# Fused attention, routed experts and a dense layer on one core: head 1's parts written in place, loads moved in the MoE

## The chip, the cores and the metric

The kernel runs on one core of a Trainium2 chip. Five engines with their own instruction streams share the work: TensorE (PE; its weight loads are shown apart as PEld), VectorE (DVE), ScalarE (ACT), GpSimd (POOL) and SyncE (SP), which here does little but issue DMAs and load registers. The metric is the device time of one execution in microseconds; the median of three executions counts.

## What is computed

Attention with rotary embedding, then a routed layer (each token goes to the best of 8 experts, chosen by the gate and a bias), then a dense layer with a gate of its own. Cut to what matters:

```python
B, H, S, D = 2, 8, 576, 64                      # 1152 tokens of 512
q, k = rotate(q), rotate(k)
attn = softmax(q @ k.T / sqrt(D)) @ v
x = attn.transpose(0, 2, 1, 3).reshape(1152, 512)
e = argmax(x @ w_gate + modality_bias[modality_id])
for each expert i, its tokens m:                # w1 8x512x1024, w2 8x1024x512
    x[m] = gate[m] * (relu(x[m] @ w1[i]) @ w2[i])
h = x @ w_in                                    # 512x2048
g = h * tanh(log1p(exp(min(h, 20))))            # h where h > 20
out = g @ w_out                                 # 2048x512
```

## The kernel before

**Arithmetic.** A float32 operand is split into a high part in the format that TensorE multiplies at full rate (`F32R`) and a low part, the rest. ScalarE or GpSimd copies the high part, VectorE or GpSimd subtracts it from the value for the low one, and a product is the sum of three matmuls (high x high, low x high, high x low). In the names `...h` or `hi` is the high part, `...l` or `lo` the low one.

**Attention** takes 16 heads `n`. For each, a load `xs` holds q (64 partitions) and k (64 partitions) with a copy of them that has its halves swapped; `p_mul` (L900) multiplies by the table of cosines and sines, `p_add` (L908) adds, `p_hi` (L920) and `p_lo` (L924) write the parts into a buffer `ab`, and `p_stack` (L930) copies `ab` with four DMAs into `sq` (q's parts above each other) and `sk` (k's parts, each on both halves of the partitions). Head 0 has a path of its own (`p_first`), in which ScalarE and VectorE write `sq` and `sk` without DMAs. Then come the scores `sc` (L963), their maximum (L973), the exponential `pexp` (L984), its transposes `pt` (L997), the parts `ph` (L1017) and `pl` (L1023), the product with v, `av` (L1038), and `xo` (L1068), which places the result in `X`. One of a head's tiles of queries is half of head n+1, so that head 0 needs head 1's `sq` and `sk`. The order of all instructions is made by the class `Plan`: a list scheduler with a key for every operation (table `K`), a cost, and counted buffers (`slots`). Of `xs` there are two buffers, and head 1's and head 2's loads come first; the scheduler has a choice of two engines for most preparing operations.

**Routing and MoE.** Each of the two batch halves `b` is routed (L313 to L524): places of the tokens are counted, GpSimd scatters the rows of `X` to a sorted array `scratch` (L408), and a table `tbl` gives for each tile its expert and first row. SP loads these numbers into registers (`tile_regs`, L552). A tile has up to 304 tokens of one expert; `moe_tile` (L673) loads 8 chunks of the expert's weights (`wraw`, L590, 0.5 MB each), ScalarE and GpSimd split them into `whi` (L598) and `wlo` (L603), and TensorE multiplies (L695). There are two tiles for each half, (0, 0), (0, 1), (1, 0) and (1, 1), and a loop L1381 over extra tiles, whose number `nxi` (L549) is computed by VectorE and loaded into a register of every engine by L1378; here it is zero and the loop's body does not run.

**The order in the MoE** comes from three generators that are advanced against each other. `pump` (L1263) advances the tiles of half 0 by `P['rq']` us of matmuls for every VectorE step of the routing of half 1. That routing ends with the register loads of the tiles of half 1, and then `merge_extra` (L526) ends with `nxi` and the DMA of `ei` into `extra`. `drive` (L1347) then runs on: `P['vl']` matmuls ahead of the register load of `nxi`, and 41 after it ahead of the loop. In `drive`, VectorE gets one decoding piece after every 24 matmuls.

**Decoding.** The dense layer's weights arrive as 16 blocks `wr` of 1 MB (`dec_load`, L1289, two buffers), of 64-bit numbers. VectorE decodes each in three pieces (L1296, L1301, L1306) into `wc`. After the third piece of block f, block f+2 is loaded:

```python
            next(d)
            if f + 2 < FC2:
                dec_load(f + 2)
```

All DMAs named here are issued by SP, one after the other in program order; an issue that waits holds those behind it.

**The last stage** takes the 16 blocks for 640 tokens and then for 512. TensorE makes `h` (L1453), ScalarE and VectorE the gate (L1464 to L1476, with a reciprocal at L1475), ScalarE and GpSimd its parts `g`, and TensorE the product `o` (L1510). The rest of the decoding pieces stand between the reciprocals.

## Time and profile before

| | before |
|---|---|
| Median of three executions | 522.54 us (521.99 to 524.20) |
| The profiled execution | 523.88 us |
| Its span, first to last instruction | 522.2 us |
| Mean granted clock of TensorE | 0.977 of full |
| Busy: TensorE, VectorE, ScalarE, GpSimd | 480.7, 409.8, 332.4, 366.3 us |

In the trace, attention ends near 172 us, the first two MoE tiles near 243, the other two near 304, and the last stage runs to the end. Busy time of TensorE is modelled for pipelined matmuls, so the time of a row of many matmuls is read from their number in a stretch. The granted clock of 1.00 is 2.4 GHz, and a stretch at the lower level shows 0.50 (1.2 GHz).

### The profile page before, as it was taken

The page shows a single profiled execution, that of the slowest core. Times are in us where ns is not written, and L with a number is a line of the kernel's source. Part 1 is how long each engine was busy: PE and PEld are TensorE (multiplying, and loading weights), DVE is VectorE, ACT ScalarE, POOL GpSimd, SP SyncE. Part 2 cuts the span into 40 slices and gives each one's busy share as a digit, 9 for nine tenths or more (in the row PEclk, how much of TensorE's full clock was granted, in tenths as well). Part 3 has the DMA queues.
Part 4 walks back from the last instruction along what each step waited for, and adds up shares of the span by engine and source line. Part 5 has one row for each costly group of instructions (what it writes and reads, how often), then busy time and mean ns, then how long its engine had stood idle before and what let it go on. Part 6 is the DMA issues. An engine that isn't in the chain of part 4 may idle for free.

```text
span 522.2 us, 9092 instructions
## 1 busy us (share of the span) xinstructions
PE 480.7 (92%) x3152; PEld 444.8 (85%) x3152; DVE 409.8 (78%) x586; ACT 332.4 (64%) x750; POOL 366.3 (70%) x359
## 2 busy tenths in 40 slices
PE   2699999999999979898999988899999899999995
PEld 1589999998988869897989987789898789999994
DVE  6489888898887665481696889999999967877773
ACT  2388788767869515454464475666666568776763
POOL 4889989999833355664777665677778558977664
PEclk9999999999999979899999999999999899999998
DMA  6588976777633684683875522022220000100001
GB/s 210 140 193 228 229 204 171 208 185 206 140 122 130 203 313 158 225 310 121 282 247 203 211 82 81 1 81 82 80 82 2 1 2 40 49 14 1 1 1 81
DMA packets 24131, 69.42 MB, mean 133 GB/s; under 512 B 5522, under 2 KB 9810, under 8 KB 22034
## 3 DMA queue, kind: packets, MB, share of 16 engines
...
q14 instruction: 23, 0.19, 0.1%
...
## 4 chain that ended last, share of the span: by engine, by line
PE 34%; DVE 12%; ACT 2%; issue 2%; POOL 2%; DMA 1%; POOLq 0%; ACTq 0%
PE h L1453 13%; PE o L1510 13%; PE mm L695 7%; DVE ta L1475 6%; DVE wc L1306 1%; DVE wc L1301 1%; DMA wraw(1, 0)_5_3587<-in_w_dram 1%; DVE yl L1401 1%; DVE ta L1476 1%; POOL wlo(1, 0)_2_3552 L603 1%; POOL wlo(1, 0)_1_3542 L603 0%; ACT w2h L1436 0%; PE mm L661 0%; DVE wc L1296 0%; POOL out_dram L1520 0%
## 5 line engine op out<-in xcount | busy, mean ns | idle before, releaser
L1475 DVE RECIPROCAL ta<-ta 128x320 f32<-128x320 f32 (+1 forms) x64 | 124.7, 1948 | 22.0 <-ACT ta L1468 20.7
L1493 POOL TENSOR_TENSOR g<-ta,g 128x320 fp32r<-128x320 f32 (+1 forms) x63 | 60.1, 954 | 61.4 <-issue 29.0
L1510 PE MATMUL o<-w2h,g 128*128 128x512 f32 x288 | 101.0, 398 | 0.0
L1437 POOL TENSOR_TENSOR w2l<-wc,w2h 128x512 fp32r<-128x512 f32 x64 | 85.7, 1360 | 3.5 <-ACT w2h L1436 3.5
L1453 PE MATMUL h<-yh,w2h 128*128 128x320 f32 (+1 forms) x256 | 76.4, 299 | 6.2 <-DVE ta L1476 6.2
L1453 PE MATMUL h<-yh,w2l 128*128 128x320 f32 (+1 forms) x256 | 76.2, 298 | 0.6 <-POOL w2l L1437 0.6
L1453 PE MATMUL h<-yl,w2h 128*128 128x320 f32 (+1 forms) x256 | 75.9, 297 | 0.2 <-DVE yl L1401 0.2
L963 PE MATMUL sc<-sk,sq 128*128 128x288 f32 (+1 forms) x320 | 59.8, 320 | 15.4 <-ACT sk L890 9.4
L984 ACT ACTIVATE pexp<-sc,nm 128x576 f32<-128x576 f32 x72 | 53.3, 741 | 24.2 <-DVE nm L973 19.3
L973 DVE TENSOR_REDUCE nm<-sc 128x1 f32<-128x576 f32 x72 | 53.5, 751 | 14.6 <-PE sc L963 11.0
L1510 PEld LDWEIGHTS o<-w2h,g 128*128 128x128 f32 x288 | 54.5, 190 | 11.0 <-POOL g L1493 1.0
L963 PEld LDWEIGHTS sc<-sk,sq 128*128 128x128 f32 (+1 forms) x320 | 47.6, 195 | 17.7 <-ACT sk L890 9.4
L1017 ACT ACTIVATE ph<-pt 128x512 fp32r<-128x512 f32 (+2 forms) x112 | 54.6, 510 | 12.2 <-PE pt L997 11.6
L1453 PEld LDWEIGHTS h<-yh,w2h 128*128 128x128 f32 x256 | 48.4, 189 | 11.1 <-DVE ta L1476 7.8
L997 PE MATMUL pt<-ident,pexp 128*128 128x128 f32 (+1 forms) x360 | 54.9, 278 | 2.7 <-DVE pl L1023 1.8
L1510 PE MATMUL o<-w2l,g 128*128 128x512 f32 x144 | 57.2, 397 | 0.0
L1487 ACT ACTIVATE g<-ta 128x320 fp32r<-128x320 f32 (+1 forms) x64 | 27.9, 436 | 41.7 <-DVE ta L1476 41.6
L1023 DVE TENSOR_TENSOR pl<-pt,ph 128x512 fp32r<-128x512 f32 (+1 forms) x80 | 48.9, 628 | 3.0 <-ACT ph L1017 2.6
L1038 PE MATMUL av<-ph,vhl 128*128 128x256 f32 (+1 forms) x160 | 50.9, 334 | 0.4 <-ACT avt L1047 0.2
L1453 PEld LDWEIGHTS h<-yl,w2h 128*128 128x128 f32 x256 | 48.3, 189 | 2.6 <-DVE yl L1401 0.4
L1453 PEld LDWEIGHTS h<-yh,w2l 128*128 128x128 f32 x256 | 48.3, 189 | 0.8 <-POOL w2l L1437 0.8
L997 PEld LDWEIGHTS pt<-ident,pexp 128*128 128x128 f32 (+1 forms) x360 | 42.1, 138 | 5.7 <-issue 2.0
...
## 6 DMA issues: line engine op xcount, KB each, us to landing
wr<-in_wio_dram SPq DMA_DIRECT2D x16, 1024.0 KB, 4.8
...
```

What stands on the lines that cost most here:

```text
L963: nc.tensor.matmul(t[:m, hf, :NC2], lhsT=sq[:, c:c + m], rhs=sk[:, z, hf * NC2:(hf + 1) * NC2], start=(z == 0), stop=(z == 1),)
L973: nc.vector.tensor_reduce(out=nm[n, j], in_=sc[n, j][:, :, :NC2], axis=AX.XY, op=ALU.max, negate=True)
L984: nc.scalar.activation(out=pe, in_=sc.pop((n, j))[:, :, :NC2], func=AF.Exp, bias=nm.pop((n, j)), accum_out=st[n, hf][:, i:i + 1],)
L997: nc.tensor.transpose(out=t[:kn, o:o + 128], in_=pexp[n, j][:, k0:k0 + kn], identity=ident)
L1017: nc.scalar.activation(out=block(ph, n, hf, kts, slice(0, kn)), in_=psum(n, hf, kts, kn), func=AF.Copy)
L1023: nc.vector.tensor_tensor(out=block(pl, n, hf, kts, slice(0, 128)) if kn == 128 else block(ph, n, hf, kts, slice(64, 128)), in0=psum(n, hf ...
L1038: nc.tensor.matmul(av[n, hf][:, :u.nq], lhsT=vhl[n][:, kt].rearrange("p a d -> p (a d)"), rhs=src[:, kt, u.at:u.at + u.nq], start=(kt == 0 ...
L1437: nc.gpsimd.tensor_tensor(out=lo[:, cs], in0=w[:, cs], in1=hi[:, cs].bitcast(F32), op=ALU.subtract)
L1453: nc.tensor.matmul(ps[:, :w], lhsT=wt[:, c], rhs=m[g, i][:, c], start=(n == 0), stop=(n == 11))
L1475: nc.vector.reciprocal(out=ta, in_=ta)
L1493: eng.tensor_tensor(out=gt[q][1][:, o:o + w], in0=tas.pop((q, i))[:, :w], in1=gt[q][0][:, o:o + w].bitcast(F32), op=ALU.subtract,)
L1510: nc.tensor.matmul(acc[g, t], lhsT=a[:, s], rhs=b, start=(f == 0 and z == 0), stop=(f == FC2 - 1 and z == 2),)
```

## The change

It has three parts.

**Head 1 in place.** For n = 1 alone, `p_hi`, `p_lo` and the four stacking DMAs are replaced. `d_hi` copies three parts on ScalarE (k, q, and `t`, which is k's second place), `d_lo` subtracts the three low parts on VectorE (GpSimd is the planner's other choice), all straight into `sq` and `sk`. `xs` gets a third buffer, free from the start, so that head 3's load is issued early.

**Register loads.** The two constants of `P` change, SP's register loads of the tiles of half 1 and the `extra` DMA move out of the routing and of `merge_extra`, and stand after a further `drive` of 24 matmuls; another 24 follow ahead of the register load of `nxi`.

**Loads of `wr`.** Until the last stage a freed buffer's load is only noted in `due`, and issued 16 matmuls after the decoding piece that freed it. From the last stage on it is issued at once.

```diff
-P = {... 'vl': 9, ... 'rq': (0.45, 0.47, 0.2), ...}
+P = {... 'vl': 24, ... 'rq': (0.52, 0.55, 0.25), ...}
...
-        nc.sync.dma_start(out=extra.rearrange("(o r) c -> o r c", o=1), in_=ei)
+        cur["ei"] = ei
...
-                [128, 2, S], F32, tag="xs" if n else "ab", name=f"xs{n}", bufs=2 if n else 1
+                [128, 2, S], F32, tag="xs" if n else "ab", name=f"xs{n}", bufs=3 if n else 1
...
+        def d_hi(n, part, eng="act"):
+            if n not in qk:
+                d_new(n)
+            sq, sk = qk[n]
+            r = slice(0, 64) if part == "q" else slice(64, 128)
+            out = {"q": sq[0:64], "k": sk[64:128, 0], "t": sk[0:64, 0]}[part]
+            if eng == "act":
+                nc.scalar.activation(out=out, in_=xin[n][r, 0], func=AF.Copy)
+            else:
+                nc.vector.tensor_copy(out, xin[n][r, 0])
+
+        def d_lo(n, part, eng="dve"):
+            sq, sk = qk[n]
+            r = slice(0, 64) if part == "q" else slice(64, 128)
+            out = {"q": sq[64:128], "k": sk[64:128, 1], "t": sk[0:64, 1]}[part]
+            hi = sq[0:64] if part == "q" else sk[64:128, 0]
+            lo_eng[eng].tensor_tensor(
+                out=out, in0=xin[n][r, 0], in1=hi.bitcast(F32), op=ALU.subtract
+            )
...
-             ... "xs": [], ...
+             ... "xs": [0.0], ...
...
-                op("phi", ("pool", "act"), (0.74, 0.573), z + pr[1], p_hi, n, deps=[("add", n)],
-                   take=[("ab", n)])
-                op("plo", ("pool", "dve"), (1.36, 0.669), z + pr[2], p_lo, n, deps=[("phi", n)],
-                   give=[("xs", n)])
-                op("stack", "sp", 2.5, z + pr[3], p_stack, n, deps=[("plo", n)], take=[("qs", n)],
-                   give=[("ab", n)], tail=2.3)
+                if n == 1:
+                    for part in "kqt":
+                        op("dhi", "act", 0.53, z + pr[1], d_hi, n, part, deps=[("add", n)],
+                           take=[("qs", n)] * (part == "k"))
+                    for part in "kqt":
+                        op("dlo", ("dve", "pool"), (0.669, 1.36), z + pr[2], d_lo, n, part,
+                           deps=[("dhi", n, "q" if part == "q" else "k")])
+                    plan.op(("stack", n), "sp", 0.0, z + pr[3], lambda: xin.pop(1),
+                            deps=[("dlo", n, x) for x in "kqt"] + [("dhi", n, "t")],
+                            give=[("xs", n)])
+                else:
+                    op("phi", ("pool", "act"), (0.74, 0.573), z + pr[1], p_hi, n, deps=[("add", n)],
+                       take=[("ab", n)])
+                    op("plo", ("pool", "dve"), (1.36, 0.669), z + pr[2], p_lo, n, deps=[("phi", n)],
+                       give=[("xs", n)])
+                    op("stack", "sp", 2.5, z + pr[3], p_stack, n, deps=[("plo", n)], take=[("qs", n)],
+                       give=[("ab", n)], tail=2.3)
...
     def route(b):
         yield from routing(b, lambda: cur["rbank"]())
-        if b:
-            tile_rows(b)
...
+    due, behind = [], [True]
+
+    def flush():
+        while due:
+            dec_load(due.pop(0))
...
-                dec_load(f + 2)
+                due.append(f + 2)
+                if not behind[0]:
+                    flush()
...
+                if nq_[0] % (3 * every) == 2 * every:
+                    flush()
...
+        drive(gen0, P["dec"][0], P["d0"], P["vl"])
+        tile_rows(1)
+        nc.sync.dma_start(out=extra.rearrange("(o r) c -> o r c", o=1), in_=cur["ei"])
...
+        behind[0] = False
+        flush()
```

The order of the instructions shows where this lands. GpSimd at the start, before, from its add of head 1 (`xs_124`) on; `xs_130` is head 2, `ab_196` the buffer that is stacked for head 1, `vhl_223` a part of v:

```order
L910 TENSOR_TENSOR xs_124<-xs_124 128x576 [waits Pool_49]
L916 TENSOR_SCALAR ab_196<-xs_124 128x576 [waits DVE_49,Pool_49]
L925 TENSOR_TENSOR ab_196<-xs_124,ab_196 128x576 [waits Pool_49]
L916 TENSOR_SCALAR vhl_223<-vraw_128 128x5x64 [waits DMAHW0_49]
L910 TENSOR_TENSOR xs_130<-xs_130 128x576 [waits DVE_49]
L1056 TENSOR_SCALAR rs_1_249<-stt 128x2 [waits Activation_49]
L916 TENSOR_SCALAR vhl_251<-vraw_187 128x5x64 [waits DMAHW4_49]
```

And after, with the parts of head 1 gone and the multiplication of head 2 (L904 of `xs_130`) come in, which VectorE did before:

```order
L910 TENSOR_TENSOR xs_124<-xs_124 128x576 [waits Pool_49]
L916 TENSOR_SCALAR vhl_198<-vraw_128 128x5x64 [waits DMAHW0_49]
L904 TENSOR_TENSOR xs_130<-xs_130,tabs 128x1152 [waits DMAHW1_49]
L910 TENSOR_TENSOR xs_130<-xs_130 128x576 [waits Pool_49]
L1082 TENSOR_SCALAR rs_1_256<-stt 128x2 [waits DVE_49,Activation_49]
L916 TENSOR_SCALAR ab_258<-xs_130 128x576 [waits DVE_49,Pool_49]
L925 TENSOR_TENSOR ab_258<-xs_130,ab_258 128x576 [waits Pool_49]
```

VectorE at the same place after the change, from the maxima of the first scores on: `xs_173` is head 3, whose multiplication stands where head 2's was before, and `sk_207` and `sq_206` are head 1's, written by the three new subtractions (L962):

```order
L999 TENSOR_REDUCE nm_4_187<-sc_111 128x1 [waits PE_49]
L999 TENSOR_REDUCE nm_3_191<-sc_110 128x1
L904 TENSOR_TENSOR xs_173<-xs_173,tabs 128x1152 [waits DMAHW4_49]
L999 TENSOR_REDUCE nm_0_214<-sc_110 128x1 [waits PE_49,Activation_49]
L962 TENSOR_TENSOR sk_207<-xs_124,sk_207 64x576 [waits DMAHW5_49,Activation_49]
L962 TENSOR_TENSOR sq_206<-xs_124,sq_206 64x576 [waits Activation_49]
L962 TENSOR_TENSOR sk_207<-xs_124,sk_207 64x576
L999 TENSOR_REDUCE nm_1_241<-sc_111 128x1 [waits PE_49]
L1049 TENSOR_TENSOR pl_1_233<-pt_1_0_209,ph_1_232 128x512 [waits Activation_49]
```

The maximum `nm_1` and the low parts `pl` now stand behind these subtractions. TensorE, before, from the transposes of head 0 to the first scores of head 1 (`sk_233`):

```order
L997 MATMUL pt_1_4_229<-ident,pexp_4_194 64x128
L1038 MATMUL av<-ph_1_215,vhl_170 128x256 [waits DVE_49,Activation_49]
L1038 MATMUL av<-pl_1_216,vhl_170 128x256 [waits DVE_49]
L1038 MATMUL av<-ph_1_215,vhl_170 128x256
L1038 MATMUL av<-pl_1_216,vhl_170 128x256
...
L1068 MATMUL xo_1_265<-mov,avt_114 128x72 [waits DMAHW3_49,DMAHW2_49,Activation_49]
L1068 MATMUL xo_1_265<-mov,avt_114 128x72
L963 MATMUL sc_110<-sk_233,sq_232 128x288 [waits DMAHW6_49,DMAHW7_49,DMAHW5_49,DMAHW0_49]
L963 MATMUL sc_110<-sk_233,sq_232 128x288
```

And after, where the scores of head 1 (`sk_207`) stand ahead of all `av` and of `xo`:

```order
L1023 MATMUL pt_1_4_229<-ident,pexp_4_196 64x128
L989 MATMUL sc_110<-sk_207,sq_206 128x288 [waits DVE_49,Activation_49]
L989 MATMUL sc_110<-sk_207,sq_206 128x288 [waits DVE_49]
L989 MATMUL sc_110<-sk_157,sq_156 64x288 x2
L989 MATMUL sc_110<-sk_207,sq_206 128x288 x2
L989 MATMUL sc_110<-sk_157,sq_156 64x288 x2
L1064 MATMUL av<-ph_1_232,vhl_170 128x256
L1064 MATMUL av<-pl_1_233,vhl_170 128x256 [waits DVE_49]
```

So nine `av` and four `xo` matmuls went behind the first scores of head 1.

SP in the MoE, before: the loads of `tbl` are the register loads of the second half's tiles, which stand between `wraw(0, 0)_5` and `_6`:

```order
L1289 DMA wr_2697<-in_wio_dram 128x2048 [waits DVE_49]
...
L590 DMA wraw(0, 0)_5_2708<-in_w_dram 128x1024 [waits DMAHW7_49,DVE_49]
L554 TENSOR_LOAD tbl_2743 [waits DVE_49]
...
L555 TENSOR_LOAD tbl_2743
...
L1289 DMA wr_2792<-in_wio_dram 128x2048
...
L590 DMA wraw(0, 0)_6_2801<-in_w_dram 128x1024 [waits DMAHW0_49,DVE_49]
L550 DMA extra<-ei 1x32 [waits DVE_49]
L1378 TENSOR_LOAD nxi [waits DVE_49]
...
L590 DMA wraw(0, 0)_7_2863<-in_w_dram 128x1024 [waits DMASW6_49,DMASW7_49,DMASW5_49,DMAHW1_49,DMASW1_49,DMASW0_49]
...
L590 DMA wraw(0, 1)_0_2908<-in_w_dram 128x1024 [waits DMAHW2_49,DVE_49,PE_49]
L1289 DMA wr_2956<-in_wio_dram 128x2048 [waits DMAHW4_49,DMAHW3_49,DVE_49]
...
L590 DMA wraw(0, 1)_1_2970<-in_w_dram 128x1024
```

And after, where each `wr` stands one chunk later or two, and the register loads behind chunk 7:

```order
L590 DMA wraw(0, 0)_5_2696<-in_w_dram 128x1024 [waits DMAHW3_49,DVE_49]
L1324 DMA wr_2715<-in_wio_dram 128x2048
...
L590 DMA wraw(0, 0)_6_2749<-in_w_dram 128x1024 [waits DMAHW4_49,DVE_49]
L1324 DMA wr_2784<-in_wio_dram 128x2048
...
L590 DMA wraw(0, 0)_7_2802<-in_w_dram 128x1024 [waits DMAHW0_49,Pool_49]
L554 TENSOR_LOAD tbl_2766 [waits DVE_49]
...
L555 TENSOR_LOAD tbl_2766
...
L1419 DMA extra<-ei 1x32 [waits DMAHW5_49,DVE_49]
...
L590 DMA wraw(0, 1)_0_2893<-in_w_dram 128x1024 [waits DMASW6_49,DMASW7_49,DMASW5_49,DMAHW6_49,DMASW1_49,DMASW0_49]
L1426 TENSOR_LOAD nxi [waits DVE_49]
...
L590 DMA wraw(0, 1)_1_2966<-in_w_dram 128x1024 [waits DMAHW7_49,DVE_49,PE_49]
...
L590 DMA wraw(0, 1)_2_2999<-in_w_dram 128x1024
```

TensorE's own register load of `nxi`, before, inside the products of chunk 3:

```order
L695 MATMUL mm_2808<-xh(0, 0)_2507,wlo(0, 0)_3_2643 128x304
L695 MATMUL mm_2808<-xh(0, 0)_2507,whi(0, 0)_3_2641 128x304
L695 MATMUL mm_2808<-xl(0, 0)_2508,whi(0, 0)_3_2641 128x304
L1378 TENSOR_LOAD nxi [waits DVE_49]
L695 MATMUL mm_2808<-xh(0, 0)_2507,wlo(0, 0)_3_2643 128x304
```

And after, 55 matmuls further on, inside those of chunk 5:

```order
L695 MATMUL mm_2899<-hh(0, 0)_2577,whi(0, 0)_5_2751 128x304
L695 MATMUL mm_2899<-hl(0, 0)_2578,whi(0, 0)_5_2751 128x304
L1426 TENSOR_LOAD nxi [waits DVE_49]
L695 MATMUL mm_2899<-hh(0, 0)_2577,wlo(0, 0)_5_2753 128x304
L695 MATMUL mm_2899<-hh(0, 0)_2577,whi(0, 0)_5_2751 128x304
```

## Rows read from the trace of the kernel before

**Rows 1.** Stretches: from:to, us; busy of PE, PEld, DVE, ACT, POOL; clock, DMA.

```profile
180.00:185.00 5.00, 5.00 (x39) 5.00 (x38) 4.73 (x18) 2.22 (x4) 3.47 (x5) 1.00 1.00 342
190.00:195.00 5.00, 5.00 (x22) 5.00 (x21) 1.90 (x4) 0.85 (x2) 2.37 (x1) 0.51 0.71 277
215.00:220.00 5.00, 4.68 (x22) 4.68 (x23) 3.01 (x5) 1.22 (x2) 5.00 (x3) 0.66 0.67 193
320.00:400.00 80.00, 76.29 (x419) 67.37 (x418) 79.28 (x69) 48.60 (x112) 53.80 (x43) 1.00 0.19 66
```

**Rows 2.** TensorE in order of time: start, us, operation, count, [idle before <-releaser].

```profile
19.35 0.56 PE L1038 MATMUL av<-ph,vhl 128*128 128x256 f32 x1
...
21.99 0.67 PE L1068 MATMUL xo<-mov,avt 128*128 128x72 f32 x4 [0.47 <-ACT avt L1047]
24.46 3.25 PE L963 MATMUL sc<-sk,sq 128*128 128x288 f32 x12 [1.81 <-DMA sk<-ab]
28.46 0.80 PE L963 MATMUL sc<-sk,sq 128*128 128x288 f32 x4 [0.76 <-ACT pexp L984]
...
189.42 0.59 PE L695 MATMUL mm<-xh(0, 0)_2507,wlo(0, 0)_3_2643 128*128 128x304 f32 x1 [3.71 <-DVE nxi L549]
```

**Rows 3.** Waits of TensorE, whole span: us in total, times, longest.

```profile
PE h L1453 <- DVE ta L1476: 6.2, 5, 1.8
...
PE mm L695 <- POOL wlo(0, 1)_1_3007 L603: 1.9, 1, 1.9
```

**Rows 4.** VectorE in order of time.

```profile
9.21 1.52 DVE L893 TENSOR_TENSOR sk<-xs,sk 64x576 fp32r<-64x576 f32 x2
...
188.44 0.14 DVE L549 TENSOR_TENSOR nxi<-nx,nx 1x1 int32<-1x1 f32 x1
...
278.78 2.40 DVE L1301 SCALAR_TENSOR_TENSOR wc<-wr,wc 128x1024 int32<-128x1024 int32 x1
```

**Rows 5.** DMA issues of SP in order of time.

```profile
204.13 0.34 SPq L1289 DMA_DIRECT2D wr<-in_wio_dram  x1
```

**Rows 6.** ScalarE in order of time.

```profile
8.71 0.68 ACT L890 ACTIVATE sk<-xs 64x576 fp32r<-64x576 f32 x1
...
188.92 1.06 ACT L598 ACTIVATE whi(0, 0)_5_2803<-wraw(0, 0)_5_2708 128x1024 fp32r<-128x1024 f32 x1 [4.27 <-DMA wraw(0, 0)_5_2708<-in_w_dram]
...
211.77 1.06 ACT L598 ACTIVATE whi(0, 1)_1_3005<-wraw(0, 1)_1_2970 128x1024 fp32r<-128x1024 f32 x1 [5.06 <-DMA wraw(0, 1)_1_2970<-in_w_dram]
```

**Rows 7.** Waits of SP's queue, 155 to 310 us: total, times, longest.

```profile
SPq L1289 <- DVE wc L1306: 42.8, 9, 10.3
...
SPq L554 <- DVE md L540: 6.8, 1, 6.8
```

**Rows 8.** GpSimd in order of time.

```profile
14.22 2.60 POOL L910 TENSOR_TENSOR xs<-xs 128x576 f32<-128x576 f32 x1
16.91 0.67 POOL L916 TENSOR_SCALAR ab<-xs 128x576 fp32r<-128x576 f32 x1
...
19.05 0.46 POOL L916 TENSOR_SCALAR vhl<-vraw 128x320 fp32r<-128x320 f32 x1
19.47 1.42 POOL L910 TENSOR_TENSOR xs<-xs 128x576 f32<-128x576 f32 x1
...
26.62 2.65 POOL L904 TENSOR_TENSOR xs<-xs,tabs 128x1152 f32<-128x1152 f32 x1
...
187.02 0.97 POOL L408 DMA_INDIRECT scratch<-X,row  x1 [0.22 <-issue]
...
277.70 2.41 POOL L603 TENSOR_TENSOR wlo(1, 1)_2_3882<-wraw(1, 1)_2_3808,whi(1, 1)_2_3880 128x1024 fp32r<-128x1024 f32 x1 [0.93 <-ACT whi(1, 1)_2_3880 L598]
```

**Rows 9.** Decoding pieces, by line: count, ns least/median/most, first and last start.

```profile
L1301 DVE SCALAR_TENSOR_TENSOR wc<-wr,wc x16: 1211/1224/2407, 194.7 to 402.1; 128x1024 int32<-128x1024 int32 x16
L1306 DVE SCALAR_TENSOR_TENSOR wc<-wr,wc x16: 1207/1800/2817, 202.5 to 404.2; 128x1024 int32<-128x1024 int32 x16
```

**Rows 10.** The page's DMA issues: count, KB each, median us to landing.

```profile
wr<-in_wio_dram SPq DMA_DIRECT2D x16, 1024.0 KB, 4.8
```

More of the change, by code (lines that the diff above doesn't have):

```diff
@@ L38 @@
 Q = {'r0': 2.45, 'rd': 2.0, 'tanh': 1.06, 'rec': 1.1, 'hi': 2.2, 'lo': 2.38, 'o': 3.86}
-P = {'sd': (3, 4), 'dl': (28, 44), 'qd': (2, 3), 'alt': (0.1, 4), 'd0': 41, 'vl': 9, 'w3': 3, 'rq': (0.45, 0.47, 0.2), 'dec': (8, 8, 8), 'rl': 3, 'ah': 0, 'eps': 0.05, 'slack': 0.1}
+P = {'sd': (3, 4), 'dl': (28, 44), 'qd': (2, 3), 'alt': (0.1, 4), 'd0': 41, 'vl': 24, 'w3': 3, 'rq': (0.52, 0.55, 0.25), 'dec': (8, 8, 8), 'rl': 3, 'ah': 0, 'eps': 0.05, 'slack': 0.1}
 K = {'ld': -22.67, 'prep': (-24.92, -22.38, -23.33, -27.14, -20.49, -7.62), 'sc': (-8.42, -3.18, 1.68, 1.67, 2.84, 10.44, 1.99, 8.05, 9.75), 'max': (-2.26, -5.46, -1.21, -1.85, 5.06, 8.41, 4.71, 11.42, 13.72), 'exp': (-3.19, 1.66, 6.32, 3.7, 13.26, 11.14, 14.6, -2.87, 25.74), 'tr': (0.69, 2.1, 2.56, 2.68, 5.53, 7.5, 8.45, 9.85, 10.88, 11.85, 15.56, 16.66, 16.92, 19.98), 'hi': (-3.91, -0.31, 2.51, 3.62, 4.25, 4.9, 5.01, 5.32, 7.26, 9.77, 13.56, 14.12, 14.6, 15.66), 'lo': (0.77, 1.83, 5.61, 6.34, 6.67, 7.32, 10.02, 10.73, 12.18, 13.92, 13.94, 14.62, 17.33, 18.02), 'pv': (7.08, 7.84, 10.5, 10.69, 14.13, 14.25, 14.32, 15.96, 18.04, 20.31, 21.03, 22.86, 23.97, 25.61), 'evac': (14.53, 9.65, 6.27, 25.13), 'rec': (-4.7, -0.45, 4.11, 12.71), 'fmm': (4.53, -3.79, 16.24, 17.22), 'norm': (15.5, 16.11, 26.18, 35.69)}
@@ L938, in p_stack, with d_new @@
             qk[n] = (sq, sk)
+        def d_new(n):
+            sq = p2.tile([128, S], F32R, tag="sq", name=f"sq{n}", bufs=3)
+            sk = p2.tile([128, 2, S], F32R, tag="sk", name=f"sk{n}", bufs=3)
+            qk[n] = (sq, sk)
+        def d_hi(n, part, eng="act"):
[16 more added lines that the diff above has]
+            )
         def v_hi(n, eng="pool"):
@@ L1096, in attention @@
             {"sc": [0.0] * 2, "pexp": [0.0] * 5, "ph": [0.0] * 2, "pha": [0.0], "av": [0.0], "qs": [0.0, 8.6],
-             "vhl": [0.0] * 2, "xs": [], "vraw": [11.9], "ab": [0.0], "avt0": [0.0],
+             "vhl": [0.0] * 2, "xs": [0.0], "vraw": [11.9], "ab": [0.0], "avt0": [0.0],
              "avt1": [0.0], "st": [0.0] * 8},
```

## The prediction

> **What bounds the kernel now.** I read the busy time by stretch first [rows 1], then what TensorE waited for [rows 2, 3], then what stood behind each wait. TensorE is the bound nearly everywhere. In an undisturbed stretch of the MoE it runs 39 matmuls of 304 columns in 5 us, 0.13 us each, at a granted clock of 1.00. In three places it is not full, and the change touches all three.
>
> First, the start. TensorE has finished head 0's early work by 22.7 us (nine `av` matmuls from 19.35, then four `xo`) and waits 1.81 us, until 24.46, for the stack DMAs of head 1 [rows 2]. The next twelve score matmuls take 3.25 us where four take 0.80 a little later, which would be 2.40 for twelve: the lower clock. One more wait of 0.76 follows at 28.46.
>
> Second, the MoE's first two tiles. TensorE stands 3.71 us until 189.42 [rows 2] for `nxi`, which VectorE writes at 188.44 [rows 4], and then gets 22 matmuls into 190 to 195, at a granted clock of 0.51, where 39 would go [rows 1]. It stands 1.9 us more for `wlo(0, 1)_1` [rows 3], and 215 to 220 again holds only 22 matmuls, clock 0.66 [rows 1]. The chain behind the second wait begins on SP's queue: the load of `wr` ahead of chunk `wraw(0, 1)_1` is issued at 204.13 [rows 5], the chunk's own right behind it, and ScalarE, idle 5.06 us for the chunk, splits it only at 211.77 [rows 6]. In 155 to 310 us SP stood 42.8 us in all before `wr` loads, for VectorE to free their buffer, and 6.8 us before the register loads of L554 [rows 7]; all that is queued behind these stood too.
>
> Third, the last stage. From 320 to 400 us VectorE is busy 79.28 of 80 us [rows 1], and TensorE's waits for L1476 come to 6.2 us [rows 3]. There VectorE is the bound.
>
> **Part 1, head 1 in place.** Before, GpSimd adds (2.60 us from 14.22, so until 16.82), makes the high part in 0.67 and subtracts [rows 8], and four DMAs stack the parts. Now three ScalarE copies of 64x576 (0.68 each [rows 6]) and three VectorE subtractions (1.52 for two, 0.76 each [rows 4]) write them, with no DMA. By these durations alone the copies run from 16.9 to 18.9 and the last subtraction is done at 19.9. TensorE has other work until 22.7, so the 1.81, the 0.76 and the 0.85 of low clock would all go: -3.4 us. That is the better bound.
>
> I don't take it, because of what GpSimd does meanwhile. The order puts the multiplication of head 2 on GpSimd right behind the add (before, VectorE did it), as one instruction, which takes 2.65 us [rows 8]. The trace shows what becomes of a two-input operation of VectorE while GpSimd is inside one. At 277.70 GpSimd starts a subtraction of 2.41 [rows 8]; VectorE's L1301 starts at 278.78, takes 2.40 and so ends 1.07 after GpSimd does [rows 4], though its median is 1.22 [rows 9]. It waited for the other's end. The opposite shows too: the add at 14.22 took 2.60, with VectorE's multiplication beside it, and the next one 1.42 [rows 8].
>
> The Trainium skill, "SBUF — State Buffer", "Who interferes with whom", has it as a rule: a VectorE instruction with two SBUF inputs and a GpSimd instruction that reads SBUF exclude each other for the whole instruction, and the order of issue decides who blocks. The rows above agree. It speaks against this part of the change: by it the part gives nothing or costs, by the lone durations it gives 3.4.
>
> So, from the rows: GpSimd's piece of `vhl` (0.46 [rows 8]) ends near 17.4, and its multiplication runs from 17.45 to 20.1. The first copy ends at 17.6, so the first subtraction comes too late by 0.2 and runs from 20.1 to 20.9. GpSimd's add for head 2 (1.42) stands ready and goes next, to 22.3; then the second and third subtraction, to 23.8, or 24.5 if GpSimd gets an instruction of 0.67 in between. Head 1 is ready at 23.8 instead of 24.46. But the order now has the nine `av` and the four `xo` behind the first scores of head 1, not ahead of them: 19.35 to 22.7 with a wait of 0.47 inside [rows 2], so 2.8 of work. Before, TensorE was through both at 30.0, which is 24.46 + 5.5, 0.8 of it the wait at 28.46. After: 23.8 + 5.5 - 0.8 + 2.8 = 31.3, and less if the 2.8 does not lie in the low clock as a whole. I take +1.0, with -3.4 (no collision) and +2.0 (third subtraction at 24.5) as bounds. Head 2's parts leave GpSimd no later than before, and the third buffer moves the load of head 3 to where TensorE waits for no DMA; both at nothing, as TensorE asks for head 2 some 9 us after head 1. Should that cover fail, it is inside the +2.0.
>
> **Part 2, register loads and `wr` loads in the MoE.** TensorE's load of `nxi` moves 55 matmuls back, to the end of chunk 5, which is 55 x 0.13 = 7.2 us of its time: 185.7 + 7.2 = 192.9, against 188.6 when the value is there. The 3.71 goes, and with it the low clock after it: 22 instead of 39 matmuls in 5 us, 17/39 x 5 = 2.2. The load itself stays on TensorE: from 188.58, when `nxi` is written [rows 4], to 189.42 it took 0.84, and that is left. What is late next is chunk 5. ScalarE got it only at 188.92, after 4.27 idle for its DMA [rows 6], which was queued behind 1 MB of `wr`, and GpSimd's last scatter ran until 188.0 [rows 8]. In the new order `wraw(0, 0)_5` stands ahead of that `wr`, so its low part is done 2.4 us after the scatter, at 190.5. TensorE comes to it 39 matmuls after the 185.7, at 190.8. That cover is thin, 0.3 us.
>
> SP's register loads of the second tile and the `extra` DMA move behind one `wr` load more and chunks 6 and 7, so these no longer stand behind VectorE. And `wr` loads are issued 16 matmuls after their buffer is free, when SP need not stand for it: `wraw(0, 1)_1` and `_2` are now ahead of the `wr` that they waited behind. The 1.9 goes, and the low clock after it: 22 matmuls in 4.68 us instead of 22 x 0.13 = 2.9, so 1.8. Sum: 3.7 + 2.2 - 0.8 + 1.9 + 1.8 = 8.8. Bounds: 5.1 (only the first wait goes, 3.7 + 2.2 - 0.8) and 9.6 (the load of the register hidden too).
>
> **Part 3, the last stage.** In the new order VectorE has one decoded piece less done when the loop begins, 10 instead of 11, and 26 instead of 27 before the first reciprocal: one more of L1306 in the stretch that VectorE bounds, 1.21 to 2.82 us, median 1.80 [rows 9]. That is +1.8. Bounds: 0, if what TensorE has queued absorbs it, and +4.0, if one of its waits grows so far that the clock falls for another 2.2, as at 190. In that stage the `wr` loads are issued at once, as before.
>
> **Sum.** -8.8 + 1.0 + 1.8 = -6.0 us. The profiled execution took 523.88 us, 1.34 above the median of 522.54 and 1.7 above its own span; 517.9 there, 516.5 at the median.
>
> **Rivals.**
> *The start pays.* If the load of head 3 or the piece of `vhl` shifts the two engines by a few tenths, the first subtraction goes ahead of the multiplication and GpSimd waits instead: -3.4 instead of +1.0, so 512.1. For it: the subtraction is late by only 0.2. Against it: both follow from the same add, which fixes their order.
> *Half of the MoE.* Chunk 5 is covered by 0.3 us, and the DMA engines are full in 180 to 185, share 1.00 at 342 GB/s [rows 1], so a later chunk may be late anyway. If one wait like the second comes back (1.9 + 1.8), the sum is -2.3: 520.2.
> *The register load still waits.* If VectorE writes `nxi` over 4 us later than now, because its routing work is pumped in another rhythm, TensorE waits at the new place and the change does not do what it says: 3.7 + 2.2 come back without the 0.8 and the sum is -0.9, 521.6. Against it: the pumping gets faster, not slower.
> *Slower.* The `wr` loads start 16 matmuls (2.1 us) later. VectorE decodes a third of one every 24 matmuls, 3.1 us, and a buffer that a third piece frees is asked for again three pieces after, 9.4 us. Less the 2.1, that leaves 7.3 us for a landing, median 4.8 [rows 10]. Where landings are longer, the decoding piece blocks VectorE, and queued behind it `hl`, for which TensorE waits. To end over 525.2, 8.7 above my sum, the nine loads that SP stood before [rows 7] would each have to be 1.0 late: landings of 8.3 us. For it: the full DMA engines at 180 to 185. Against it: that is one stretch, not nine.
>
> **How the numbers follow.** The forecast (514 to 519) 0.45; the start pays 0.22; half of the MoE 0.18; register load 0.08; slower 0.07. The range for 8 in 10 goes from 511.5, where the start pays and the MoE gives its 9.6, to 521.5, which leaves out the slower case and part of the register's. About 0.5%, 2.6 us, is what a measurement here can tell from no change: 519.9 to 525.2. Faster by more: 0.45 + 0.22 + 0.08 of the half case = 0.75. Within: 0.10 + 0.08 = 0.18. Slower: 0.07.
>
> **What would show it.** Right: no TensorE wait for `nxi`, clock 1.00 at 190 to 195, no wait for `wlo(0, 1)_1`; the first subtraction of head 1 lasting over 2 us beside GpSimd's multiplication, and head 1's first score at 23.5 to 24.5; the last stage's VectorE as full as now. Wrong: subtractions of 0.76 each and scores of head 1 before 21 (the start pays); a new TensorE wait for a `wlo` of chunks 5 to 7, or for `hl` behind a late decoding piece.

## The result and the profile after

The change takes 516.58 us (median; 515.54 to 518.28) where the kernel before, run beside it, takes 522.26 (519.96 to 524.2): a ratio of 0.9896, 95% interval 0.9867 to 0.9925, or 5.7 us less. The forecast was 516.5. The profiled execution took 515.94, its span is 514.2; before it was 523.88 and 522.2, so the two spans differ by 8.0, more than the medians.

Where the 8.0 went is read by marks that both traces have, in TensorE's and VectorE's order of time (start, us, operation): the first MoE matmul, the first matmul behind the MoE loop, the first reciprocal of the last stage, and the last matmul that waited for VectorE's `ta`. Before:

```profile
172.44 0.41 PE L695 MATMUL mm<-xh(0, 0)_2507,whi(0, 0)_0_2348 128*128 128x304 f32 x1
...
244.84 0.41 PE L695 MATMUL mm<-xh(1, 0)_3274,whi(1, 0)_0_3302 128*128 128x304 f32 x1 [2.07 <-issue]
...
307.51 2.15 DVE L1475 RECIPROCAL ta<-ta 128x320 f32<-128x320 f32 x1 [0.65 <-ACT ta L1468]
...
408.61 0.42 PE L1453 MATMUL h<-yh,w2h 128*128 128x320 f32 x1 [1.77 <-DVE ta L1476]
```

After:

```profile
172.90 0.41 PE L695 MATMUL mm<-xh(0, 0)_2506,whi(0, 0)_0_2338 128*128 128x304 f32 x1
...
236.50 0.41 PE L695 MATMUL mm<-xh(1, 0)_3272,whi(1, 0)_0_3300 128*128 128x304 f32 x1 [2.14 <-issue]
...
298.58 2.15 DVE L1523 RECIPROCAL ta<-ta 128x320 f32<-128x320 f32 x1 [0.65 <-ACT ta L1516]
...
402.52 0.42 PE L1501 MATMUL h<-yh,w2h 128*128 128x320 f32 x1 [1.77 <-DVE ta L1524]
```

The differences of neighbouring marks, in us, with the span's end as the last mark:

| stretch | before | after | change |
|---|---|---|---|
| start: to the first MoE matmul | 172.44 | 172.90 | +0.46 |
| MoE: to the matmul behind the loop | 72.40 | 63.60 | −8.80 |
| behind the loop: to the first reciprocal | 62.67 | 62.08 | −0.59 |
| VectorE-bound: to the last wait for `ta` | 101.10 | 103.94 | +2.84 |
| tail: to the end | 113.59 | 111.68 | −1.91 |

The MoE pays, the stretch that VectorE bounds gives a third of it back. The −0.59 and the −1.91 lie where TensorE's work is the same. In the tail the clock fell in the trace before and not in the one after. Behind the loop it fell in both; of the −0.59, 0.3 is a wait of TensorE for `hl(1, 0)` that the trace before has there and the one after has not. Busy time by stretch (from:to, us; busy of PE, PEld, DVE, ACT, POOL; clock, DMA) before:

```profile
237.00:253.00 16.00, 13.93 (x89) 13.69 (x88) 2.94 (x5) 5.40 (x9) 9.56 (x4) 0.89 0.42 134
400.00:420.00 20.00, 18.23 (x92) 15.77 (x92) 18.83 (x14) 11.83 (x28) 13.30 (x12) 0.91 0.00 2
```

and after:

```profile
190.00:195.00 5.00, 4.72 (x34) 4.47 (x33) 3.03 (x9) 1.39 (x2) 0.26 (x1) 1.00 1.02 422
215.00:220.00 5.00, 5.00 (x38) 5.00 (x37) 3.26 (x4) 2.73 (x5) 4.96 (x2) 1.00 1.01 356
228.00:245.00 17.00, 14.86 (x96) 14.61 (x95) 5.64 (x6) 5.97 (x9) 9.00 (x4) 0.90 0.50 159
400.00:420.00 20.00, 18.23 (x108) 16.16 (x107) 17.53 (x14) 13.22 (x30) 12.69 (x12) 1.00 0.00 0
```

At 400 to 420 the granted clock was 0.91 before and 1.00 after, with the program shifted by some six us. Without these two stretches the sum is 0.46 − 8.80 + 2.84 = −5.5, with the −0.59 it is −6.1: the median's −5.7 lies between them. The other rows answer to [rows 1]: 190 to 195 holds 34 matmuls at 1.00 where it held 22 at 0.51, 215 to 220 holds 38 where it held 22, and VectorE is as full from 320 to 400 as it was (79.25 of 80 us, before 79.28).

TensorE's waits after (total, times, longest) answer to [rows 3]:

```profile
PE h L1501 <- DVE ta L1524: 6.7, 5, 1.8
PE sc L989 <- DVE sq L962: 2.9, 1, 2.9
...
PE sc L989 <- DMA sk<-ab: 1.1, 1, 1.1
...
PE mm L695 <- DVE hl(0, 0)_2578 L720: 0.3, 1, 0.3
```

The waits for `nxi` and for `wlo(0, 1)_1` are gone. The one for head 1's stack has become a longer one for the new subtractions, and a wait of 1.1 for head 2's stack is new. Another of 0.3, for `hl(0, 0)`, is new.

### The profile page after: what moved, and what is told of

Same layout as the page of the kernel before. It is cut to its first block, busy times and chain, and to the rows that moved or that the text cites. A ratio compares the mean times of both kernels' runs of the same rounds, so it can differ in the third digit from the quotient of the medians.

```text
span 514.2 us, 9105 instructions
## 1 busy us (share of the span) xinstructions
PE 476.0 (93%) x3152; PEld 438.2 (85%) x3152; DVE 411.8 (80%) x589; ACT 334.5 (65%) x753; POOL 366.6 (71%) x357
## 4 chain that ended last, share of the span: by engine, by line
PE 31%; DVE 18%; issue 3%; ACT 1%; POOL 0%; POOLq 0%
DVE ta L1523 11%; PE mm L695 11%; PE h L1501 10%; PE o L1558 10%; DVE wc L1336 2%; DVE ta L1524 1%; DVE yl L1449 1%; DVE wc L1331 1%; DVE wc L1341 1%; PE mm L661 0%; POOL out_dram L1568 0%; POOLq L1692 0%; DVE idi L1636 0%; ACT ot L1564 0%; ACT ta L1513 0%
## 5 line engine op out<-in xcount | busy, mean ns | idle before, releaser
L1541 POOL TENSOR_TENSOR g<-ta,g 128x320 fp32r<-128x320 f32 (+1 forms) x63 | 57.7, 916 | 62.0 <-issue 31.1
L1485 POOL TENSOR_TENSOR w2l<-wc,w2h 128x512 fp32r<-128x512 f32 x64 | 88.9, 1411 | 3.4 <-ACT w2h L1484 3.4
L1501 PEld LDWEIGHTS h<-yh,w2h 128*128 128x128 f32 x256 | 48.2, 188 | 11.9 <-DVE ta L1524 9.1
```

Source lines behind the costliest of these rows:

```text
L1485: nc.gpsimd.tensor_tensor(out=lo[:, cs], in0=w[:, cs], in1=hi[:, cs].bitcast(F32), op=ALU.subtract)
L1501: nc.tensor.matmul(ps[:, :w], lhsT=wt[:, c], rhs=m[g, i][:, c], start=(n == 0), stop=(n == 11))
L1541: eng.tensor_tensor(out=gt[q][1][:, o:o + w], in0=tas.pop((q, i))[:, :w], in1=gt[q][0][:, o:o + w].bitcast(F32), op=ALU.subtract,)
```

## The experiments

Each is the changed kernel with one edit. All are told by the same five stretches, with the decoding pieces that VectorE has done before the first reciprocal; the ratio is to the kernel before on the same chip.

| kernel | start | MoE | behind | VectorE-bound | tail | pieces | median | ratio, interval |
|---|---|---|---|---|---|---|---|---|
| before | 172.44 | 72.40 | 62.67 | 101.10 | 113.59 | 27 | 522.3 | 1 |
| after | 172.90 | 63.60 | 62.08 | 103.94 | 111.68 | 26 | 516.58 | 0.9896 (0.9867–0.9925) |
| x1 | 173.50 | 70.71 | 65.11 | 101.11 | 113.17 | 27 | 521.88 | 0.9975 (0.994–1.0009) |
| x2 | 172.83 | 63.11 | 60.83 | 103.92 | 113.51 | 26 | 515.46 | 0.9828 (0.9764–0.9892) |
| x3 | 170.05 | 64.28 | 60.85 | 103.94 | 113.58 | 26 | 515.9 | 0.9866 (0.9804–0.9929) |
| x4 | 175.04 | 68.80 | 62.07 | 101.12 | 111.97 | 27 | 518.42 | 0.9917 (0.9881–0.9953) |
| y1 | 171.80 | 62.48 | 60.86 | 103.96 | 113.70 | 26 | 515.97 | 0.9889 (0.9825–0.9953) |
| y2 | 174.43 | 62.72 | 60.90 | 103.95 | 113.20 | 26 | 517.84 | 0.9896 (0.9858–0.9934) |
| y3 | 173.45 | 63.14 | 60.54 | 103.93 | 111.94 | 26 | 517.79 | 0.991 (0.9881–0.9939) |
| y4 | 172.28 | 64.34 | 60.83 | 101.16 | 113.19 | 27 | 515.13 | 0.9867 (0.9806–0.9929) |
| z0 | 172.22 | 62.44 | 62.08 | 103.92 | 111.64 | 26 | 514.71 | 0.9871 (0.9833–0.9909) |
| z1 | 174.57 | 65.61 | 60.87 | 101.87 | 113.68 | 27 | 515.2 | 0.9858 (0.9795–0.992) |
| z3 | 173.53 | 63.52 | 62.08 | 101.09 | 111.98 | 27 | 514.03 | 0.983 (0.9753–0.9907) |

(Before stands with its first trace, and a median as in the batch of x1; z0 is the changed kernel itself, once more beside z1 to z3; z2 has other marks and is told last.)

### Which part pays

The four kernels x1 to x4 hold one part of the change, or two.

**x1**, head 1 alone: the two constants of `P`, the register loads, the `extra` DMA and the `wr` loads are as before (the lines of the register loads and of `extra` are left out here).

```diff
-P = {... 'vl': 24, ... 'rq': (0.52, 0.55, 0.25), ...}
+P = {... 'vl': 9, ... 'rq': (0.45, 0.47, 0.2), ...}
...
-    due, behind = [], [True]
+    due, behind = [], [False]
```

> The kernel before with part 1 alone: head 1's parts written in place, third xs buffer; register loads and wr loads as before. The collision theory (VectorE's subtractions wait for GpSimd's multiplication, head 2's stack is late behind the load of head 4): TensorE waits about 2.9 us for the subtractions and 1.1 us for head 2's stack, the first MoE matmul comes 0 to 1 us later than before, and the time is +0.5 us against before (0 to +1.5). The rival, that the start pays and another part of the change eats it: -3 us.

**x2**, everything but head 1:

```diff
-                if n == 1:
-                    for part in "kqt": ...
-                else:
+                if True:
...
-                [128, 2, S], ... bufs=3 if n else 1
+                [128, 2, S], ... bufs=2 if n else 1
...
-             ... "xs": [0.0], ...
+             ... "xs": [], ...
```

> The changed kernel without part 1: register loads and wr loads moved, heads as before. If the MoE gives 8.8 us and the last stage takes 1 to 3 back, independent of the start: -6 to -7.5 us against before, no TensorE wait for nxi, none for a wlo of the second tile's chunk 1, first MoE matmul where it was before. The rival, that part 1 carries a share of the gain: -3 us only.

**x3**, the register loads alone: x2, and `wr` loads at once.

```diff
-    due, behind = [], [True]
+    due, behind = [], [False]
```

> Register loads and their two constants moved, but a freed wr is loaded at once, as before; heads as before. If the two parts of the MoE term are separate: the first wait goes (3.7 + 2.2 - 0.8 = 5.1) and the wait for the second tile's chunk 1 with its low clock (3.7) stays, last stage +1 to +2: -3 to -4 us. The rival, that the later wr loads do nothing: as the run with both, -6 to -7.5. Another rival, that without them chunk 5 is late: a new wait in place of the nxi one, -1.

**x4**, the later `wr` loads alone: x2, with register loads and `P` as before.

> The wr loads 16 matmuls later, register loads and heads as before. If the parts are separate: the wait for nxi stays with its low clock, the wait for the second tile's chunk 1 goes with its own: -3.7 us. The rival, that SP's register loads hold the chunks by themselves: 0 us, with the wait for the second tile's chunk 1 as before.

x1 takes 0.4 us off, with an interval on both sides of 1, and x2 without head 1 is no slower than the whole change: head 1 in place is worth nothing that can be measured in the time. The MoE's 8.8 is in x2 as in the change. Its parts don't add up, though: x3 alone has −8.1, x4 alone −3.6, together 11.7 where x2 has −9.3. x4 keeps the wait of 3.7 for `nxi` (TensorE's waits):

```profile
PE mm L695 <- DVE nxi L549: 3.7, 1, 3.7
```

and takes off what the sum gave to the second wait, 1.9 + 1.8. But x3, which issues `wr` loads at once, loses the second wait too. SP's issues in x3 show why:

```profile
194.44 0.33 SPq L590 DMA_DIRECT2D wraw(0, 1)_1_2967<-in_w_dram  x1
...
198.66 0.34 SPq L1314 DMA_DIRECT2D wr<-in_wio_dram  x1
```

With the register loads moved, one decoding piece less is done by then, so the `wr` load that stood ahead of `wraw(0, 1)_1` at 204.13 [rows 5] stands behind it already. Either edit removes the second wait; the later `wr` loads add 1.2 to what the registers bring (64.28 to 63.11). In x3 TensorE waits 1.2 for `hl(0, 1)`, in x2 it does not; the two totals alone could not tell it, since the changed kernel itself has 63.60 in one trace and 62.44 in the other (z0).

x1's MoE is 1.7 shorter although its order there is that of before. Its second wait is short:

```profile
PE mm L695 <- POOL wlo(0, 1)_1_3006 L603: 0.6, 1, 0.6
```

It was 1.9 [rows 3], and from 215 to 220 x1 has 36 matmuls at a granted clock of 1.00. So this wait and the low clock behind it can be nearly absent in a trace without any edit in the MoE; x1 gives 1.2 of it back in a wait for `hl(0, 1)`. Behind the loop x1 is 2.4 longer, with a wait of 2.4 for `hl(1, 0)`, whose cause stays open.

### What the start does with its gain

VectorE after, in order of time (a maximum of head 0's scores, then the three subtractions):

```profile
16.59 0.74 DVE L999 TENSOR_REDUCE nm<-sc 128x1 f32<-128x576 f32 x1
17.36 2.85 DVE L962 TENSOR_TENSOR sk<-xs,sk 64x576 fp32r<-64x576 f32 x1
20.25 1.84 DVE L962 TENSOR_TENSOR sq<-xs,sq 64x576 fp32r<-64x576 f32 x1
22.11 0.75 DVE L962 TENSOR_TENSOR sk<-xs,sk 64x576 fp32r<-64x576 f32 x1
```

ScalarE's first copy of head 1:

```profile
15.80 0.68 ACT L953 ACTIVATE sk<-xs 64x576 fp32r<-64x576 f32 x1
```

GpSimd in the same stretch, the add of head 1, the piece of `vhl`, then multiplication and add of head 2:

```profile
14.05 1.40 POOL L910 TENSOR_TENSOR xs<-xs 128x576 f32<-128x576 f32 x1
15.42 1.57 POOL L916 TENSOR_SCALAR vhl<-vraw 128x320 fp32r<-128x320 f32 x1
16.96 2.63 POOL L904 TENSOR_TENSOR xs<-xs,tabs 128x1152 f32<-128x1152 f32 x1
19.67 1.80 POOL L910 TENSOR_TENSOR xs<-xs 128x576 f32<-128x576 f32 x1
```

And TensorE:

```profile
22.23 0.41 PE L989 MATMUL sc<-sk,sq 128*128 128x288 f32 x1 [2.89 <-DVE sq L962]
22.92 2.05 PE L989 MATMUL sc<-sk,sq 128*128 128x288 f32 x7 [0.29 <-DVE sk L962]
...
28.36 0.78 PE L989 MATMUL sc<-sk,sq 128*128 128x288 f32 x4
...
33.74 0.77 PE L989 MATMUL sc<-sk,sq 128*128 128x288 f32 x4 [1.13 <-DMA sk<-ab]
```

The last of these scores, before:

```profile
33.38 0.77 PE L963 MATMUL sc<-sk,sq 128*128 128x288 f32 x4
```

The collision is there. The first subtraction, 0.76 when alone [rows 4], ends at 20.21, that is 0.62 after GpSimd's multiplication; the second, 1.84 long, ends 0.62 after GpSimd's add; the third has no partner and takes 0.75. TensorE gets head 1 at 22.23 instead of 24.46, with the `av` and `xo` behind it. By 28.36 it has started 32 score matmuls, 16 transposes, the nine `av` and the four `xo` since the beginning; before, it was there at 30.00, with three transposes more. At 0.1 us for a transpose (nine took 0.9 before, from 29.10) it is some 1.3 us ahead, an estimate. Then it waits 1.13 for head 2, and at the scores behind this wait it is 0.36 behind: they start at 33.74 where it was 33.38, with the same number of matmuls of each kind done. SP after, in order of time:

```profile
24.94 0.33 SPq L863 DMA_DIRECT2D xs<-in_qk_dram  x1
25.32 0.53 SPq L934 DMA_DIRECT2D sq<-ab  x1
...
27.18 0.60 SPq L937 DMA_DIRECT2D sk<-ab  x1
```

and its waits from 8 to 40 us:

```profile
SPq L863 <- POOL ab L925: 11.9, 1, 11.9
```

SP stood 11.9 us before the load of head 4, whose buffer head 2 frees last of all (L925), and head 2's four stacking DMAs are queued behind that load. **y1** puts them ahead of it:

```diff
-                op("load", "sp", 0.45, ..., p_load, n, take=[("xs", n)], ...)
+                op("load", "sp", 0.45, ..., p_load, n, take=[("xs", n)], ...,
+                   deps=[("stack", 2)] * (n == 4))
```

> The changed kernel, with the load of head 4 put behind the stacking DMAs of head 2 in SP's order. If head 2's stack is late because it stands behind that load, which SP held 11.9 us for GpSimd: the 1.1 us wait of TensorE for the stack goes, the stack's first DMA is issued near 23.5 instead of 25.3, and the first MoE matmul comes about 1 us earlier than in the changed kernel (172.9). The rival, that the stack is late for GpSimd's sake: the wait stays, 0.

SP in y1, and under it TensorE:

```profile
23.41 0.53 SPq L934 DMA_DIRECT2D sq<-ab  x1
```

```profile
33.09 0.77 PE L989 MATMUL sc<-sk,sq 128*128 128x288 f32 x4
```

The stack's first DMA starts 1.9 earlier, its last one 1.1 earlier, and they land sooner. From issue to landing the two DMAs into `sk` took, in z0, which is the changed kernel again (the trace of after does not have their landing):

```profile
DMA to landing us min/median/max: 5.5/5.9/6.3
```

and in y1:

```profile
DMA to landing us min/median/max: 3.2/3.7/4.1
```

x2, with the heads as before, and z2, with y1's edit, have 3.2 to 4.1 too; y4, without it, has 5.3 to 6.0. Against the kernel before, the change does not issue the stack late (25.32 to 27.18, where it was 25.19 to 27.85). It lands late, with the 576 KB of head 4 issued 0.4 us ahead of it.

In y1 the wait is gone, and the MoE begins 1.1 earlier than in the profile of after. That the load ahead of the stack makes it land late is shown; a gain in time is not. z0 began its MoE at 172.22. y4 below, whose start is that of after, began it at 172.28 and did not wait for the stack either, because TensorE came to these scores later. And the medians lie too close.

**y2** splits the multiplication of head 2 into four pieces, as head 1's is, so that VectorE gets a turn in between:

```diff
-... if n == 1 else (slice(0, S),):
+... if n < 3 else (slice(0, S),):
...
-... if n == 1 else (slice(0, 2),):
+... if n < 3 else (slice(0, 2),):
```

> The changed kernel, with GpSimd's multiplication of head 2 as four instructions of a quarter each. If VectorE and GpSimd exclude each other for whole instructions and take turns: the first subtraction of head 1 waits for one quarter (0.66) and takes about 1.4 us instead of 2.85, the last one ends near 21.3 instead of 22.9, GpSimd's multiplication stretches by the subtractions in it, and TensorE's first score of head 1 comes about 1.5 us earlier. The rival, that they only share bandwidth: the three subtractions take 5.4 us together as before.

GpSimd, VectorE and TensorE in y2:

```profile
17.11 4.60 POOL L904 TENSOR_TENSOR xs<-xs,tabs 128x288 f32<-128x288 f32 x4
```

```profile
17.51 1.00 DVE L962 TENSOR_TENSOR sk<-xs,sk 64x576 fp32r<-64x576 f32 x1
18.54 1.24 DVE L962 TENSOR_TENSOR sq<-xs,sq 64x576 fp32r<-64x576 f32 x1
19.81 1.23 DVE L962 TENSOR_TENSOR sk<-xs,sk 64x576 fp32r<-64x576 f32 x1
```

```profile
21.06 2.29 PE L989 MATMUL sc<-sk,sq 128*128 128x288 f32 x8 [1.38 <-DVE sk L962]
...
34.89 1.30 PE L989 MATMUL sc<-sk,sq 128*128 128x288 f32 x4 [2.78 <-DMA sk<-ab]
```

The engines take turns instruction by instruction: the subtractions end at 21.04 instead of 22.86, GpSimd's four pieces take 4.60 instead of 2.63. What head 1 gains, head 2 loses: TensorE waits 2.78 for its stack, and the MoE begins at 174.43. **y3** gives head 2's multiplication to VectorE and head 3's to GpSimd:

```diff
+                if n in (2, 3):
+                    e = "dve" if n == 2 else "pool"
+                    op("mul", e, 1.27 if n == 2 else 2.67, ..., lambda n, e=e: p_mul(n, e), ...)
...
```

> The changed kernel, with the multiplication of head 2 on VectorE and that of head 3 on GpSimd, as before the change. The collision theory: only GpSimd's add of head 2 (1.4) can stand ahead of the subtractions; they end near 20.5, scores of head 1 start 2 us earlier than in the changed kernel, head 2's stack is issued some 3 us earlier and not waited for; first MoE matmul 2 to 3 us earlier than 172.9. The rival, that something else at the start (DMA, the low clock) takes it back: within 1 us.

ScalarE and TensorE in y3:

```profile
16.52 0.68 ACT L953 ACTIVATE sk<-xs 64x576 fp32r<-64x576 f32 x1 [5.21 <-POOL xs L910]
```

```profile
19.53 1.33 PE L989 MATMUL sc<-sk,sq 128*128 128x288 f32 x4 [6.92 <-ACT pexp L1010]
```

The expected 2 to 3 us did not come. Head 2's stack is issued from 21.71 on and TensorE does not wait for it. But the planner put a maximum of head 0's scores behind VectorE's multiplication (13.57 to 15.24), and ScalarE's three copies of head 1 ahead of `pexp`. The copies waited 5.21 for GpSimd's add, which took 2.39 beside that multiplication; `pexp` came at 18.64, and TensorE stood 6.92 in one wait. The MoE began at 173.45.

### What the last stage costs

**y4** puts a decoding piece back ahead of the loop:

```diff
         drive(gen0, P["dec"][0], P["d0"], P["vl"])
+        decode(1)
         tile_rows(1)
```

> The changed kernel, with one decoding piece more on VectorE after the first 24 matmuls, so that 27 are done before the first reciprocal, as before the change. If the missing piece is what makes the stretch from the first reciprocal to TensorE's last wait for VectorE 103.9 us instead of 101.1: it is 101.1 again, and the time is 2 to 2.8 us less than the changed kernel's, as the piece lies beside TensorE's work in the MoE. The rival, that the longer stretch comes from another phase of GpSimd and VectorE: 103.9 stays, or the piece costs the MoE what it gives (0).

The VectorE-bound stretch is 101.16, as before the change; in every kernel here it is 101.1 to 101.2 with 27 pieces done and 103.9 with 26 (101.87 in z1, with 27). But the piece costs in the MoE, where `hl(0, 1)` is now waited for 0.9 us: 64.34 against 62.44 to 63.60. The expected 2 to 2.8 us of time are not shown: the median of 515.13 lies too close to the changed kernel's (516.58, and 514.71 in z0).

### Amendments together

**z0** is the changed kernel, unchanged. **z1** is y1 and y4 together, **z3** is x2 and y4, and **z2** is z1 with a 28th piece behind the loads, at the place right ahead of the loop where VectorE idles:

```diff
         n_extra = nc.values_load(nx, ...)
         drive(gen0, P["dec"][0], P["d0"])
+        flush()
+        decode(1)
```

> The changed kernel again, beside the three others: the stretches that no chance touches should repeat, 63 to 64 us from the first MoE matmul to the first one behind the loop and 103.9 from the first reciprocal to TensorE's last wait for VectorE, while the start and the two places where the clock may or may not fall (behind the loop, and behind that last wait) may differ by 1 to 2 us each. 516 to 517.

> The changed kernel with both amendments: head 4's load behind head 2's stack, one decoding piece more ahead of the loop. If they add up: -1 at the start, -2.8 in the last stage, up to +0.7 in the MoE for the piece, so 513 to 514, 3 under the changed kernel beside it. The rival, that the two only move chance: as the changed kernel.

> As the one with both amendments, and a 28th piece right ahead of the loop, where VectorE is idle for 5 us. If every piece less in the last stage is worth its own length: another -1 to -2 from the first reciprocal to TensorE's last wait (99 to 100). The rival, that it is the phase against GpSimd which counts: 101 or more again.

> Without part 1 (heads as before the change), with the moved loads of the MoE and the one piece more. If part 1 is worth nothing: 513 to 514, as the version with both amendments, 101.1 from the first reciprocal to the last wait. The rival, that head 1 in place with the stack mended is worth its 1 us: 1 us above that version.

z1 missed: its start was 174.57 and its MoE 65.61, and its 515.2 is no better than either edit alone. Its profiled execution was the slowest of four (518.61, the others 513.68 to 515.37). TensorE stands 2.13 us there ahead of scores at 44.15, for which the profile shows no releaser and y1, with the same start, has no counterpart. z3 has the 27 pieces and no head 1: 514.03. z2 is the fastest: 512.46 (510.7 to 512.49; ratio 0.9815, 0.9754 to 0.9876), each of its times under each of z0's (513.27 to 519.54). VectorE in z2, the added piece (L1342) and what follows it:

```profile
226.75 1.36 DVE L1342 SCALAR_TENSOR_TENSOR wc<-wr,wc 128x1024 int32<-128x1024 int32 x1
237.87 0.47 DVE L720 SCALAR_TENSOR_TENSOR hl(1, 0)_3545<-mm,hh(1, 0)_3544 128x304 fp32r<-128x304 f32 x1 [9.76 <-ACT hh(1, 0)_3544 L718]
```

and TensorE's waits for VectorE in its last stage:

```profile
PE h L1505 <- DVE ta L1528: 4.0, 4, 1.6
```

The piece stands in a gap that is still 9.76 long behind it. From the first reciprocal to the end z2 takes 212.4, where it is 213.1 to 215.6 with 27 pieces and 215.6 to 217.7 with 26, and the waits for `ta` fall from 6.7 to 4.0. Part of these ranges is the clock. Among the traces with a granted clock of 1.00 from 400 to 420, it is 215.6 to 215.9 with 26 pieces (after, z0, y3), 213.1 with 27 (x4, z3) and 212.4 with 28. So the 27th piece is worth 2.5 there and the 28th 0.7. That is a version which beats both kernels.

## Why the prediction was right, and where its steps were not

**The MoE, −8.8, measured −8.80.** The sum was right and its split was not. The clock and both waits went as forecast: 34 and 38 matmuls where there were 22, at 1.00. What failed is the step that gave the first wait's 5.1 to the register load and the second's 3.7 to the later `wr` loads. The 3.7 comes out as 3.6 in x4, but x3 shows that the register part alone removes both, and x1 that most of it can be missing with no edit there at all.

Inside the 8.8, the 0.84 of the register load that the sum kept as left failed too. VectorE and GpSimd after:

```profile
190.78 0.14 DVE L549 TENSOR_TENSOR nxi<-nx,nx 1x1 int32<-1x1 f32 x1
```

```profile
187.38 2.40 POOL L603 TENSOR_TENSOR wlo(0, 0)_5_2753<-wraw(0, 0)_5_2696,whi(0, 0)_5_2751 128x1024 fp32r<-128x1024 f32 x1
```

`nxi` is written at 190.78, 2.3 later than before [rows 4], within the 4 us that the rival allowed. TensorE's matmuls run on at 0.14 us each from 191.75 to 194.94, all through chunk 5, with no gap, so a register load whose value is there was hidden, 0.8 less than forecast: the bound of 9.6 is the better sum, of which the new wait for `hl(0, 0)` takes 0.3. x2's MoE has 9.3 less than before, and the kernels with both edits and no added piece lie at 62.4 to 63.6, the 63.60 of this pair at the upper end. Chunk 5's low part ended at 189.78 (forecast 190.5), and TensorE did not wait for it. That rival, half of the MoE, did not come.

**Head 1, +1.0, measured +0.46 in this pair, −0.4 in x1's median.** The collision came, in the turns that were worked out. The Trainium skill, "SBUF — State Buffer", "Who interferes with whom", says that a VectorE instruction with two SBUF inputs and a GpSimd instruction that reads SBUF contend for one exclusive lock. The trace agrees, with 2.85 us for the first subtraction.

That the subtraction came behind the multiplication is luck. The forecast had it late by 0.2 because of GpSimd's add; but the add took 1.40, not 2.60, and the first copy was done at 16.48, 0.48 before the multiplication began. What held the subtraction to 17.36 was VectorE's maximum ahead of it, which the forecast did not count. The sizes were off too. GpSimd's multiplication began at 16.96, not 17.45, and the third subtraction had no partner. Head 1 was whole at 22.86, not 23.8, and TensorE's first score could start without the third part, at 22.23, earlier than the 23.5 to 24.5 that were to show the forecast right. From there to the mark of 30.0 the sum had 7.5 us; to the same work the trace has some 6.4 (22.23 to 28.36, and three transposes). So at this mark the change was some 1.3 ahead where 1.3 behind was forecast.

The step that failed is the one that took the third buffer and head 2's parts "both at nothing". The prediction watched head 3's load, which does go early. But with that buffer taken early the load of head 4 became the one that has to wait, and it stands ahead of head 2's stack on SP. It held SP for 11.9 us, the DMAs into `sk` landed 5.5 to 6.3 us after their issue (z0) where 3.2 to 4.1 is seen without it (y1, x2), and 1.13 of TensorE's lead went in the wait. The cover of "some 9 us" was counted from TensorE's side, with no price for a late landing.

By the end of attention +0.46 is left, less than the scatter of the start. At an equal granted clock the traces with head 1 in place begin the MoE 2.2, 0.5 and 0.7 later, and in one case 0.2 earlier (table in the last section): a cost, as forecast, but each from one pair of traces. One price in the bound of −3.4 was low: x3 ran the twelve scores in 1.85 us at a clock of 1.00, not 2.40, so the low clock cost 1.4 there and not 0.85.

**The last stage, +1.8, measured +2.84.** The mechanism, one piece less before the first reciprocal, is shown by y4. The term was mis-sized: the price of a piece was taken as one median, 1.80 [rows 9], but the pieces also fell into another phase against GpSimd. Decoding pieces after (count, ns least/median/most):

```profile
L1336 DVE SCALAR_TENSOR_TENSOR wc<-wr,wc x16: 1211/1977/3222, 191.9 to 396.1; 128x1024 int32<-128x1024 int32 x16
L1341 DVE SCALAR_TENSOR_TENSOR wc<-wr,wc x16: 1217/1355/3314, 201.4 to 398.1; 128x1024 int32<-128x1024 int32 x16
```

The medians were 1.224 and 1.800 [rows 9]; they are 1.977 and 1.355, so one of the pieces collides more and the other less. That the phase is the whole of the other 1.0 is argued, not shown. It stayed under the bound of +4.0.

**The sum.** −8.8 + 0.46 + 2.84 = −5.5 against −6.0: half of the 1.0 that the last stage cost more was made good at the start. The forecast was the likeliest case and it came. That 516.5 and 516.58 lie so close is luck: two terms missed by −0.5 and +1.0, and the same changed kernel has a median of 514.71 in z0. The start did not pay in time, though it did give TensorE head 1 early; the slower case needed late `wr` landings that hold up `hl`, and all that TensorE waited for `hl` in the first two tiles is the 0.3.
